# Four-token query runs, decay moved from keys to values, and another schedule in a fused linear-attention and sine-MLP kernel

## The chip, the cores and the metric

One core of a Trainium2 chip runs the whole program in one launch. The metric is device microseconds of that core, the median of several runs.

## The reference, cut to what matters

```python
# q, k, v: (4, 8, 768, 64) f32; lam: (8,)
for b in range(12):                                   # blocks of 64 tokens
    intra = einsum('bhic,bhjc->bhij', qb, kb) * Dmask # lam**(i-j) for i >= j, else 0
    intra = einsum('bhij,bhjd->bhid', intra, vb)
    inter = einsum('bhid,bhde->bhie', qb * lam**(pos+1), kv_state)
    out[block] = intra + inter
    kv_state = lam**64 * kv_state + einsum('bhsd,bhse->bhde', kb * lam**(63-pos), vb)
x = out as (3072 tokens, 512)
h = x @ w_in                                          # w_in (512, 2048)
g = h + sin(alpha*h)**2 / (alpha + 1e-9)
return g @ w_out                                      # (2048, 512), f32 out
```

## The kernel before, in words

**Tiling.** Attention runs in 24 blocks of 128 tokens (4 batches of 6), all 8 heads at once; the MLP in 6 chunks of 512 tokens, 4 blocks each. The decays are taken out of the score matrix: q is multiplied by `Lq` = lam to the token's place in its batch (L464), k by `Lk` = lam to minus that place (L471), so scores need a 0/1 mask only and the state needs no decay of its own. Both products go to bf16 into `qk2`; v is cast to `v2` (L473).

**Attention, per block s.** `piece_Q` (L506) and `piece_T` (L488) transpose q and k on TensorE (PE) through PSUM, and L511 and L493 copy them to `qkT`; from block `TD` = 12 on, a DMA transpose on SP's queue (L479) does both instead. `part_S` (L543) makes scores of all heads in two banks, DVE masks them into `Sm` (L552). `part_Z` (L568) accumulates the state in bank 7, copied to `Zc` (L583) or from block 12 on to the block-diagonal `Zd` (L578). `part_O` (L616 or L603, then L623) makes the output, copied to `xT` (L632), the MLP's input. q is loaded for two blocks at once, two neighbouring tokens of a head per partition, runs of 512 bytes; k and v in runs of 256 bytes.

**MLP.** A hidden unit (`unit_A`, L671, 4 matmuls of 512 columns; `unit_A2`, L705, two hidden tiles of 256 columns) fills a PSUM bank; ACT takes the sine (L681, L715), POOL or ACT the square (L686, L720 and L685, L719; one source line calls either engine), DVE adds (L688, L723) into `gT`. `unit_B` (L736) multiplies four hidden tiles by `w_out`; after four of them ACT copies the bank to `osb` (L749) and a store goes out (L751).

**Loads.** SP asks for q, k, v of blocks 0 to 3 first, then the first 512 columns of w_in in f32 into `ws`, which DVE casts (L391). The other three quarters of w_in and four quarters of w_out are cast by POOL's own DMA queue; `load_w1(i, [last["k32", 3]])` and the wait of `load_q(4, [last["w1", 2]])` tie them to the arrival of k of block 3, and of the third quarter of w_in (index 2). All loads are issued on line 342.

**Order.** `_Plan` records every operation with a cost and its tiles; `_settle` and `_order` choose for each engine an order (and an engine, where two are offered) by a list schedule over these costs, and `emit` writes the instructions with semaphores. PE may take any of the next 40 operations, SP only the next. A filler (`spin`, L829) multiplies unused data while PE would idle ahead of the first hidden unit.

Of the kernel before, what the change touches and what calls it, by code (L numbers as in the profile page):

```python
# [13 lines left out]
class _Op:  # L14


    def __init__(self, eng, emit, dur, reads, writes, dma, after, issue, lat, runs=64):
        self.eng, self.emit, self.dur = eng, emit, dur
        self.given = eng
        self.issue, self.lat, self.runs = issue, lat, runs  # L20
        self.lead = 0
        self.reads, self.writes, self.dma = reads, writes, dma
        self.port = False
        self.after = after
        self.deps = set()
        self.needed = False
        self.count = None
        self.start = None
        self.done = None
        self.knows = None  # L30


class _Plan:

    AHEAD = {"PE": 40, "SP": 1}
    SLACK = 0.3  # L40
    EARLY = 0.0, 0.0

    LAT = 0.2
# [10 lines left out]
    def op(self, eng, emit, dur, reads=(), writes=(), dma=None, after=(), issue=0.4, lat=2.6, runs=64):  # L54
# [14 lines left out]
        o.deps.discard(o)  # L69
        o.lead = self.lead  # L70
# [4 lines left out]
    def _transfers(order):  # L75
# [5 lines left out]
        left = {e: [[o.start + 0.8, o.runs, o.dur / o.runs, o] for o in sorted(q, key=lambda o: o.start)]  # L81
# [19 lines left out]
    def _settle(self):  # L101

        filler, lands, best = self.filler, {}, None
        for _ in range(8):
            self.filler = filler
            for o in self.ops:
                o.eng, o.start, o.done = o.given, None, None
            order = self._order(lands)
            new = self._transfers(order)
            off = sum(abs(t - o.done) for o, t in new.items())  # L110
            state = [(o, o.eng, o.start, o.done) for o in order]
            if best is None or off < best[0]:
                best = off, order, state
# [5 lines left out]
    def _order(self, lands):  # L119
        index = {o: i - o.lead for i, o in enumerate(self.ops)}  # L120
        left = {}
        for o in self.ops:
            left.setdefault(o.eng if isinstance(o.eng, str) else "any", []).append(o)
        fixed = {e: left.pop(e, []) for e in ("PE", "SP")}
        free = [o for e in left for o in left[e]]
        clock = {e: 0.8 for e in ("PE", "SP", "ACT", "DVE", "POOL")}
        wire = 0.0
        port = 0.0
        order = []

        def ready(o):
            t = 0.0
            for d in o.deps:
                if d.done is None:
                    return None
                t = max(t, d.done + (0.0 if d.eng == o.eng else self.LAT))
            return t

        while fixed["PE"] or fixed["SP"] or free:
            best = None  # L140
            for e in ("PE", "SP"):
                can = []
                for o in fixed[e][:self.AHEAD[e]]:
                    r = ready(o)
                    if r is not None:
                        can.append((max(r, clock[e]), index[o], o, e, o.dur))
                if can:
                    soon = min(c[0] for c in can)
                    soon += self.EARLY[1] if e == "PE" and soon < self.EARLY[0] else self.SLACK
                    c = min((c for c in can if c[0] <= soon), key=lambda c: c[1])  # L150
                    if best is None or c[:2] < best[:2]:
                        best = c
            for o in free:
                r = ready(o)
                if r is None:
                    continue
                if o.port:
                    r = max(r, port)
                if isinstance(o.eng, str):
                    c = (max(r, clock[o.eng]), index[o], o, o.eng, o.dur)  # L160
                else:
                    _, e, d = min((max(r, clock[e]) + d + late, e, d) for e, d, late in o.eng)
                    c = (max(r, clock[e]), index[o], o, e, d)
                if best is None or c[:2] < best[:2]:
                    best = c
            t, _, o, e, dur = best
            if e == "PE" and self.filler is not None:
                emit, reads, last = self.filler
                if last.start is not None:
                    self.filler = None  # L170
                else:
                    deps = [self.writer[b] for b in reads]
                    at = max([clock["PE"]] + [d.done + self.LAT if d.done is not None else t for d in deps])
                    n = int((t - at) / 0.4)
                    if n > 0:
                        f = _Op("PE", lambda h, n=n: emit(h, n), 0.4 * n, tuple(reads), (), None, (), 0, 0)
                        f.deps = set(deps)
                        f.start, f.done = at, at + 0.4 * n
                        order.append(f)
            if isinstance(o.eng, str):  # L180
                (fixed[e] if e in fixed else free).remove(o)
            else:
                free.remove(o)
                o.eng = e
            o.start = t
            if o.dma is not None:
                clock[e] = t + o.issue
                wire = max(wire, t + 0.8) + dur
                o.done = max(t + 0.8 + o.dur + o.lat, lands[o]) if o in lands else wire + o.lat
            else:  # L190
                clock[e] = o.done = t + dur
                if o.port and e != "ACT":
                    port = o.done
            order.append(o)
        return order
# [48 lines left out]
def bass_lightning_attn__then__act_snake_kernel(  # L244
# [26 lines left out]
    TD = 12  # L271
# [5 lines left out]
    RU = 4  # L277

    es = contextlib.ExitStack()
    with es:  # L280
# [18 lines left out]
        q32 = ring("q32", RL // 2, [128, H, 2, D], F32)  # L299
# [8 lines left out]
        mask = sb("mask", [128, 8, 128], BF16)  # L308
        maskf = sb("maskf", [128, 128], F32)
# [4 lines left out]
        E_i = sb("E_i", [128, 2 * NB, H], I32)  # L314
        E_f = sb("E_f", [128, 2 * NB, H], F32)
        lnL = sb("lnL", [128, 2 * NB, H], F32)
        Lq = sb("Lq", [128, NB, H], F32)
# [12 lines left out]
        def _(_unused_eng):  # L330
# [5 lines left out]
            P.EARLY = 20.0, 0.3  # L336
# [4 lines left out]
            def load(dst, src, key, dur, sem, eng="SP", lat=2.6, after=(), issue=0.4, runs=64):  # L341
# [3 lines left out]
            def load_q(s, after=()):  # L345
# [3 lines left out]
                for lo, hi in ((0, 4), (4, H)) if s < 4 else ((0, H),):  # L349
                    last["q32", s] = load(  # L350
                        q32[j][:, lo:hi, :, :].rearrange("p h t d -> p h (t d)"),
                        q[b, lo:hi, n * BL:(n + 2) * BL, :].rearrange("h (p t) d -> p h (t d)", t=2),
                        [("q32", j, a) for a in range(lo // 4, hi // 4)],
                        (0.9 if s == 0 else 1.1 if s < 4 else 2.3), f"q32{j}" + (str(lo) if s < 4 else ""),
                        lat=2.7, after=after, runs=8 * (hi - lo),
                    )

            def load_kv(s, which="kv"):
                b, n, j = s // NB, s % NB, s % RL
                for nm, src, dst in (("k32", k, k32), ("v32", v, v32)):  # L360
                    if nm[0] in which:
# [3 lines left out]
                            (nm, j), 1.1, f"{nm}{j}", lat=2.7,  # L365
# [7 lines left out]
            def load_w1(i, after):  # L373
# [3 lines left out]
                    [("w1", 2 * i), ("w1", 2 * i + 1)], 2.55, f"w1{i}", "POOL", 3.8, after, 0.8, 32,  # L377
                )

            def load_w1_first():  # L380
                for lo in (0, 256):
# [3 lines left out]
                        ("ws", lo), 1.65, f"ws{lo}", lat=2.7, runs=32,  # L385
# [8 lines left out]
            def load_w2(i, after):  # L394
# [3 lines left out]
                    [("w2", 2 * i), ("w2", 2 * i + 1)], 2.55, f"w2{i}", "POOL", 3.8, after, 0.8, 32,  # L398
# [3 lines left out]
            load(lam_bc[:, :], bass.AP(lam.tensor, 0, [[0, 128], [1, H]]), "lam", 0.1, "lam", "ACT", runs=1)  # L402
            load(alphaT[:, :], bass.AP(moe_alpha.tensor, 0, [[128, NM], [1, 128]]), "alphaT", 0.1, "alphaT", "ACT", lat=4.9, runs=1)
# [5 lines left out]
            load_q(2)  # L409
# [9 lines left out]
            op("POOL", lambda e: e.tensor_copy(E_f[:, :, :], E_i[:, :, :]), 0.3, ["E_i", "E_k"], ["E_f"])  # L419
# [5 lines left out]
            op("DVE", lambda e: e.memset(maskf[:, :], 1.0), 0.2, writes=["maskf"])  # L425
            op("POOL", lambda e: e.affine_select(
                out=maskf[:, :], in_=maskf[:, :], pattern=[[1, 2], [2, 64]], compare_op=ALU.is_ge,
                fill=0.0, base=0, channel_multiplier=-1), 0.5, ["maskf"], ["maskf"])
            op("DVE", lambda e: e.tensor_copy(mask[:, :, :], bass.AP(maskf, 0, [[128, 128], [0, 8], [1, 128]])),  # L429
               0.8, ["maskf"], ["mask"])  # L430

            for i in range(2):
# [3 lines left out]
            lnlam_b = bass.AP(lnlam, 0, [[H, 128], [0, 2 * NB], [1, H]])  # L436
            op("DVE", lambda e: e.tensor_tensor(lnL[:, :, :], E_f[:, :, :], lnlam_b, ALU.mult), 0.2,
               ["E_f", "lnlam"], ["lnL"])
            op("ACT", lambda e: e.activation(Lq[:, :, :], lnL[:, 0:NB, :], ACTF.Exp), 0.3, ["lnL"], ["Lq"])
            op("ACT", lambda e: e.activation(Lk[:, :, :], lnL[:, NB:2 * NB, :], ACTF.Exp, scale=-1.0), 0.3,  # L440
               ["lnL"], ["Lk"])
            op("ACT", lambda e: e.activation(warm[:, :], lnlam[:, 0:1], ACTF.Sin, scale=0.0), 1.5,
               ["lnlam", "Lk"], ["warm"])
# [7 lines left out]
            def QE(s, a):  # L451
                return "DVE" if (s, a) in () else "POOL"
# [5 lines left out]
            def scale_block(s):  # L458
# [3 lines left out]
                for a in range(2) if s % 2 == 0 else ():  # L462
                    ported(op(QE(s, a),
# [466 lines left out]
```

## Time and profile before

| | |
|---|---|
| runs | 222.61, 223.09, 224.41 us (median 223.09) |
| profiled run | 223.52 us, span 221.4 us, granted clock 1.00 |
| PE | busy 208.6 us, 94% of the span, 1645 matmuls |
| ACT, DVE, POOL | 155.9, 122.6, 89.1 us (70, 55, 40%) |
| DMA | 33.31 MB, mean 150 GB/s; 63520 packets under 512 B |
| PE idle | 5.6 us before 20 us, 4.6 us from there to the last matmul, 2.6 us after it |

Busy time counts instructions on the engine; a busy PE need not be at its peak. In the timeline each row is start, length, engine, line, operation, output and inputs, count, and in brackets the idle time ahead of it and what ended it. In the table of windows the columns are the stretch, its length, then busy time (and instructions) of PE, weight loads, DVE, ACT and POOL, the granted clock, the DMA share and GB/s.

### The profile page before, as it was taken

The numbers are of one execution on the slowest core, as the hardware profiler recorded it, in microseconds if no ns is written. First come the engines' busy times: TensorE is split into PE (matmuls) and PEld (weight loads), VectorE is DVE, ScalarE is ACT, GpSimd is POOL, SyncE is SP. The second block draws the span as 40 slices with busy tenths as digits, with TensorE's granted clock in tenths as the row PEclk, the third lists the DMA queues.
The fourth block names the chain that finished last, engine by engine and source line by source line (L and its number), as shares of the span: only waits on it lengthen the run. The fifth ranks groups of instructions, "written<-read, shape, count | busy, mean of one in ns | idle before, by whom it ended". The sixth has DMA issues, their size and how long they took to land.

```text
span 221.4 us, 4062 instructions
## 1 busy us (share of the span) xinstructions
PE 208.6 (94%) x1645; PEld 110.7 (50%) x1645; DVE 122.6 (55%) x184; ACT 155.9 (70%) x277; POOL 89.1 (40%) x100
## 2 busy tenths in 40 slices
PE   3889987899898999999999999999999999999995
PEld 1446433456575785545445444545545444444444
DVE  4687775354777887667655455645465544445100
ACT  3735994347697997788788887877788677778211
POOL 4386763454978776863576103011001011110100
DMA  5999999999999999999999752110110011101112
GB/s 131 236 232 271 206 214 208 217 235 237 233 245 275 242 191 245 219 254 189 276 240 245 155 112 33 47 50 0 47 50 21 26 47 50 47 0 49 75 70 95
DMA packets 83651, 33.31 MB, mean 150 GB/s; under 512 B 63520, under 2 KB 80688, under 8 KB 83632
## 3 DMA queue, kind: packets, MB, share of 16 engines
q1 hardware_dynamic: 76880, 24.25, 53.6%
q0 software_dynamic: 3696, 3.67, 9.9%
q10 hardware_dynamic: 3056, 5.13, 6.4%
q8 instruction: 13, 0.21, 0.4%
q14 instruction: 6, 0.05, 0.1%
HBM read 27.28 MB, written 6.29 MB: 152 GB/s over the span
## 4 chain that ended last, share of the span: by engine, by line
PE 63%; DMA 24%; POOL 4%; SPq 4%; ACT 2%; DVE 1%; issue 1%
PE bank L736 32%; PE bank L671 24%; DMA k<-in_k_dram 10%; DMA q<-in_q_dram 5%; DMA v<-in_v_dram 4%; DMA w<-in_moe_w_in_dram 4%; SPq L342 4%; PE bank L705 3%; PE bank L623 2%; PE bank L543 2%; POOL qk L471 1%; POOL qk L464 1%; PE bank L603 1%; POOL u L720 1%; DVE gT L723 1%
## 5 line engine op out<-in xcount | busy, mean ns | idle before, releaser
L736 PE MATMUL bank<-w,gT 128*128 128x512 bf16 (+1 forms) x400 | 94.8, 371 | 0.0
L688 DVE SCALAR_TENSOR_TENSOR gT<-u,rinv,bank 128x512 bf16<-128x512 bf16 x74 | 54.6, 746 | 51.7 <-ACT u L685 34.2
L671 PE MATMUL bank<-xT,w 128*128 128x512 bf16 x296 | 74.2, 379 | 0.6 <-DVE gT L688 0.6
L681 ACT ACTIVATE t<-bank,alpha 128x512 bf16<-128x512 f32 x74 | 50.6, 686 | 24.1 <-PE bank L671 24.0
L736 PEld LDWEIGHTS bank<-w,gT 128*128 128x128 bf16 x400 | 37.7, 98 | 39.6
L686 POOL TENSOR_TENSOR u<-t 128x512 bf16<-128x512 bf16 x19 | 19.7, 1040 | 80.7 <-ACT t L681 79.7
L671 PEld LDWEIGHTS bank<-xT,w 128*128 128x128 bf16 x296 | 28.5, 98 | 34.9 <-DVE gT L688 1.1
L685 ACT ACTIVATE u<-t 128x512 bf16<-128x512 bf16 x55 | 34.4, 629 | 1.8 <-DVE gT L723 0.3
L552 DVE TENSOR_TENSOR Sm<-bank,mask 128x1024 bf16<-128x1024 f32 x24 | 29.2, 1222 | 10.3 <-PE bank L568 7.7
L464 POOL TENSOR_TENSOR qk<-q,Lq 128x512 bf16<-128x512 f32 x24 | 24.5, 1044 | 21.7 <-DMA q<-in_q_dram 18.1
L471 POOL TENSOR_TENSOR qk<-k,Lk 128x512 bf16<-128x512 f32 x22 | 22.9, 1044 | 7.2 <-DMA k<-in_k_dram 7.0
L749 ACT COPY osb<-bank 128x512 f32<-128x512 f32 (+1 forms) x25 | 14.2, 569 | 14.8 <-PE bank L736 14.8
L705 PE MATMUL bank<-xT,w 128*128 128x256 bf16 x176 | 22.3, 273 | 2.0 <-DVE gT L723 2.0
L723 DVE SCALAR_TENSOR_TENSOR gT<-u,rinv,bank 128x256 bf16<-128x256 bf16 x44 | 19.1, 476 | 7.2 <-POOL u L720 4.1
L715 ACT ACTIVATE t<-bank,alpha 128x256 bf16<-128x256 f32 x44 | 18.5, 471 | 3.3 <-PE bank L705 3.1
L705 PEld LDWEIGHTS bank<-xT,w 128*128 128x128 bf16 x176 | 16.2, 98 | 5.5 <-DVE gT L723 3.0
L473 ACT CAST v<-v 128x512 bf16<-128x512 f32 x18 | 11.0, 615 | 7.6 <-DMA v<-in_v_dram 7.6
L632 ACT CAST xT<-bank 128x512 bf16<-128x512 f32 (+1 forms) x18 | 12.9, 716 | 2.8 <-PE bank L568 1.6
L720 POOL TENSOR_TENSOR u<-t 128x512 bf16<-128x512 bf16 x11 | 11.3, 1039 | 4.7 <-ACT t L715 4.6
L543 PE MATMUL bank<-qkT 64*128 64x128 bf16 x192 | 9.8, 226 | 0.2 <-DVE qkT L493 0.2
L623 PE MATMUL bank<-Sm,v 128*64 128x128 bf16 x192 | 9.9, 225 | 0.0
L829 PE MATMUL bank<-mask,ident 128*128 128x512 bf16 x12 | 5.7, 564 | 3.7 <-DVE mask L429 3.7
(55 smaller groups left out, 111.4 us busy)
## 6 DMA issues: line engine op xcount, KB each, us to landing
k<-in_k_dram SPq DMA_DIRECT2D x24, 256.0 KB, 5.5
v<-in_v_dram SPq DMA_DIRECT2D x24, 256.0 KB, 5.5
q<-in_q_dram SPq DMA_DIRECT2D x10, 512.0 KB, 5.5
out_dram<-osb ACTq DMA_DIRECT2D x19, 256.0 KB, 2.0
w<-in_moe_w_out_dram POOLq DMA_DIRECT2D x4, 512.0 KB, 13.1
w<-in_moe_w_in_dram POOLq DMA_DIRECT2D x3, 512.0 KB, 9.0
q<-in_q_dram SPq DMA_DIRECT2D x4, 256.0 KB, 4.6
ws<-in_moe_w_in_dram SPq DMA_DIRECT2D x2, 512.0 KB, 5.4
```

Of the source, the lines that this page charges most:

```text
L464: lambda e, a=a: e.tensor_tensor(qk2[:, j:j + 2, 4 * a:4 * a + 4, :], q32[jq][:, 4 * a:4 * a + 4, :, :].rearrange("p h t d -> p t h d"), b ...
L471: lambda e: e.tensor_tensor(qk2[:, j, H:2 * H, :], k32[jl][:, :, :], lk, ALU.mult), 0.7 if s in (0,1) else 1.05,
L552: op("DVE", lambda e: e.tensor_tensor(Sm[s % 2][:, :, :], banks[:, 512 * b0:512 * b0 + 1024].rearrange("p (c i) -> p c i", i=128), mask[:, ...
L671: ins = e.matmul(ps[hb][:, c0:c1], w1[:, kc, 128 * m:128 * (m + 1)], xT[x][:, kc, c0:c1], start=(kc == 0 and c0 == lo), stop=(kc == NKC - ...
L681: op("ACT", lambda e: e.activation(t16[ju][:, w], ps[hb][:, w], ACTF.Sin, scale=alpha[:, m:m + 1]), 0.69 * f, [bank(hb), "alpha"], [("t16" ...
L685: lambda e: (e.activation(u16[ju][:, w], t16[ju][:, w], ACTF.Square) if e is nc.scalar else e.tensor_tensor(u16[ju][:, w], t16[ju][:, w], ...
L686: e.tensor_tensor(u16[ju][:, w], t16[ju][:, w], t16[ju][:, w], ALU.mult)), 0,
L688: op("DVE", lambda e: e.scalar_tensor_tensor(out=gT[g][:, m, w], in0=u16[ju][:, w], scalar=rinv[:, m:m + 1], in1=ps[hb][:, w], op0=ALU.mul ...
L705: ins = e.matmul(ps[hb][:, 256 * i:256 * i + 256], w1[:, kc, 128 * (m + i):128 * (m + i + 1)], xT[x][:, kc, lo:lo + 256], start=(kc == 0 a ...
L715: op("ACT", lambda e, i=i: e.activation(t16[ju][:, 256 * i:256 * i + 256], ps[hb][:, 256 * i:256 * i + 256], ACTF.Sin, scale=alpha[:, m + ...
L723: op("DVE", lambda e, i=i: e.scalar_tensor_tensor(out=gT[g][:, m + i, lo:lo + 256], in0=u16[ju][:, 256 * i:256 * i + 256], scalar=rinv[:, ...
L736: ins = e.matmul(ps[ob][:, w], gT[g][:, m, 128 * s4:128 * (s4 + 1)], w2[:, m, w], start=(m == 0), stop=(m == NM - 1),)
```

## The change

q of blocks 0 to 3 is loaded in two pieces of four heads for all four blocks, four neighbouring tokens per partition (runs of 1024 bytes); its own decay table `Lq4`, its own mask, and strides of four in scores and outputs follow. DVE multiplies these four blocks' q. From block 4 on, and for blocks 0 and 1, the decay `Lk` goes into v and k is only cast; blocks 2 and 3 keep it in k. `TD` goes from 12 to 10. The mask is stored once and read with a stride of zero over the 8 heads. The fillers use 256 columns of a tile set at the start. The planner gets other costs, hand-over times by engine, windows of choice by engine, and a list of priority shifts; the four stores of chunk 0 are recorded later, after the pieces of blocks 8 to 11. The three w_in requests of POOL stand in one run, as before.

```diff
-    AHEAD = {"PE": 40, "SP": 1}
-    SLACK = 0.3
-    LAT = 0.2
+    AHEAD = 40
+    WINDOW = {"PE": 0.3, "ACT": 0.1, "DVE": 0.1, "POOL": 0.1}
+    PIPE = {"ACT": 0.11, "DVE": 0.09, "POOL": 0.045, "PE": 0.0}
+    HOP = {"PE": 0.055, "ACT": 0.035, "DVE": 0.035, "POOL": 0.075, "SP": 0.1}
+    DRAIN = 0.085
+    MOVES = (
+        (500, 10, "all", -75), (367, 10, "all", -265), (210, 3, "all", -185), (249, 30, "all", 55),
+        (294, 3, "ACT", 60), (111, 1, "SP", -10), (239, 30, "all", -40), (396, 1, "SP", 5),
+        (94, 10, "SP", -10), (244, 1, "ACT", -20),
+    )
...
+        prio = {o: i - o.lead for i, o in enumerate(self.ops)}
+        for at, width, kind, by in self.MOVES:
+            for o in self.ops[at:at + width]:
+                if (kind == "all" and o.given != "SP") or o.given == kind or ...:
+                    prio[o] += by
...
-    TD = 12
+    TD = 10
+    QD = ((0, 0), (0, 2), (1, 0), (1, 2))
...
+                if s < 4:
+                    for a in range(2):
+                        last["q32", s] = load(
+                            q32[:, a, :, :, :].rearrange("p (h x) t d -> p h (x t d)", x=2),
+                            q[0, 4 * a:4 * a + 4, 0:4 * BL, :].rearrange("h (p t) d -> p h (t d)", t=4),
+                            [("q32", a, 0), ("q32", a, 1)], 1.66, f"q32{a}", lat=1.4, after=after, runs=32,
+                        )
+                    return
...
-            load_q(2)
...
+                if s == 0:
+                    for a in range(2):
+                        for t in (0, 2):
+                            ported(op(QE(a, t),
+                               lambda e, a=a, t=t: e.tensor_tensor(
+                                   qk2[:, t:t + 2, 4 * a:4 * a + 4, :],
...
-                ported(op("DVE" if s in (0,1) else "POOL",
-                   lambda e: e.tensor_tensor(qk2[:, j, H:2 * H, :], k32[jl][:, :, :], lk, ALU.mult), 0.7 if s in (0,1) else 1.05,
-                   [("k32", jl), "Lk"], [("k2", j)]))
-                op((("ACT", 0.62, 0.0), ("POOL", 1.05, 0.3)) if s > 11 else "ACT", lambda e: ... v2[j] <- v32[jl] ...
+                plain, decayed = ((kj, k32[jl], ("k32", jl), ("k2", j)), (vj, v32[jl], ("v32", jl), ("v2", j)))[::1 if s < 2 or s > 3 else -1]
+                ported(op("POOL", lambda e: e.tensor_tensor(decayed[0], decayed[1][:, :, :], lk, ALU.mult), 1.05,
+                          [decayed[2], "Lk"], [decayed[3]]))
+                op((("ACT", 0.62, 0.0), ("POOL", 0.62, 0.3)) if s > 11 else "ACT",
+                   lambda e: (e.copy if e is nc.scalar else e.tensor_copy)(plain[0], plain[1][:, :, :]), 0.62,
+                   [plain[2]], [plain[3]])
...
+            def queries(s):
+                nq = 4 if s < 4 else 2
+                w = BL // nq
+                return s % RT // nq * nq, nq, slice(w * (s % nq), w * (s % nq) + w)
...
-                    for ahead in range(s + 2, min(s + 3, NBLK)) if s >= 10 else ():
+                    for ahead in range(s + 2, min(s + 3, NBLK)) if s >= 8 else ():
...
             piece_Q(0, 4)
+            piece_Q(2, 6)
...
-            piece_Q(2, 4)
...
-                    ins = e.matmul(ps[0][:, :], ident[:, :], mask[:, 0:4, :].rearrange("p a b -> p (a b)"))
+                    ins = e.matmul(ps[0][:, 0:256], idle[:, 0:128], idle[:, :])
...
-            load_pair(10)
...
-            for st in stores:
-                if st is not None:
-                    st("SP")
             pieces = pieces_of(8, None, False) + pieces_of(10, 9, False)
...
             prep(13)
+            for st in stores:
+                if st is not None:
+                    st("SP")
```

More of the change, by code (lines that the diff above doesn't have):

```diff
@@ L101, in _settle @@
     def _settle(self):
[L103 to L111, printed above, removed]
+        prio = {o: i - o.lead for i, o in enumerate(self.ops)}
+        for at, width, kind, by in self.MOVES:
+            for o in self.ops[at:at + width]:
+                if (kind == "all" and o.given != "SP") or o.given == kind or (kind == "any" and not isinstance(o.given, str)):
+                    prio[o] += by
+        lands, best = {}, None
+        for _ in range(10):
+            order, new, off = self._pass(prio, lands)
             if best is None or off < best[0]:
-                best = off, order, state
+                best = off, order, [(o, o.eng, o.start, o.done) for o in order]
+            if off < 0.5:
+                break
             lands = new
@@ L117, in _settle, with _pass @@
         return best[1]
[L119 to L121 removed]
+    def _pass(self, prio, lands):
         for o in self.ops:
[L123 to L168 removed]
@@ L194, in _order @@
             order.append(o)
+            can.discard(o)
+            left -= 1
+            for s in after.get(o, ()):
+                waits[s] -= 1
+                if not waits[s]:
+                    can.add(s)
         return order
@@ L835, in _ @@
                 if i == 0:
[L836 removed]
+                    P.filler = (spin, ("idle",), u)
                 if i == 3:
```

260 lines of the change are left out of this document (164 added, 96 removed).

## The prediction

> **What bounds the kernel now.** I read the busy tenths first, then TensorE's (PE's) waits, then the chain that ended last, then the timeline at the places these name. The busy tenths give two stages.
>
> ```profile
> PE   3889987899898999999999999999999999999995
> DMA  5999999999999999999999752110110011101112
> ```
>
> One digit is 5.5 us. PE is full from the fifth digit on except for dents near 36 and 55 to 66 us, while the DMA engines are saturated until about 120 us. So the end is a sum of PE work, and time can only go where PE still waits, or where PE work itself goes. The waits of PE between 19 and 100 us are these (us in total, times, longest):
>
> ```profile
> PE bank L705 <- DVE gT L723: 2.0, 3, 1.0
> PE bank L506 <- POOL qk L464: 1.7, 1, 1.7
> PE bank L671 <- DVE gT L688: 0.6, 1, 0.6
> PE bank L488 <- POOL qk L471: 0.2, 1, 0.2
> ```
>
> 4.5 us in all. The chain shows what stands behind the second and fourth (start, us, what):
>
> ```profile
> 9.09 5.78 DMA k<-in_k_dram
> ...
> 14.93 1.04 POOL qk L471
> 15.97 0.88 POOL w L342
> 16.85 9.00 DMA w<-in_moe_w_in_dram
> ...
> 26.28 16.12 DMA k<-in_k_dram
> ```
>
> k of block 3 lands at 14.93, POOL scales it, only then asks for w_in; the second w_in part lands at 25.85, only then SP asks for q, k, v of blocks 4 and 5, and those crawl behind the weight loads. PE meets that at 39.31:
>
> ```profile
> 16.80 2.35 DVE L552 TENSOR_TENSOR Sm<-bank,mask 128x1024 bf16<-128x1024 f32 x2
> 19.89 1.92 PE L705 MATMUL bank<-xT,w 128*128 128x256 bf16 x16
> 38.21 2.04 POOL L464 TENSOR_TENSOR qk<-q,Lq 128x512 bf16<-128x512 f32 x2 [2.23 <-DMA q<-in_q_dram]
> 39.31 0.40 PE L506 MATMUL bank<-ident,qk 128*128 128x128 bf16 x4 [1.72 <-POOL qk L464]
> ```
>
> The first MLP matmul (L705) starts at 19.89, right after the last score mask on DVE (16.80 to 19.15). From 90 us PE does not wait, so the last 130 us are PE work alone.
>
> **Parts of the change, one by one.**
>
> *q of blocks 0 to 3 in 1 KB runs.* The same 1 MB, 1024 packets for 2048. In the trace's packet records a 512 B packet took 31 ns in the mean, and ws (w_in's first columns, 1 KB packets) 55 ns, at the fast end 46. Over 16 engines: 2048 x 31 / 16 = 3.97 us against 1024 x 46..55 / 16 = 2.94 to 3.5 us, so 0.45 to 1.0 us of engine time. Packets overlap (busy shares of about 1.2 in these windows), so elapsed 0.4 to 0.85; I take 0.65. k3, ws and w_in all stand behind these q loads in the queue and land so much earlier. The price: k0 now stands behind 1 MB of q, not 0.5 MB, some 1.7 us later; the queue has paid that back by k2, because q of blocks 2 and 3 was in front of it before.
>
> [...]
>
> *Work moved between engines in the head.* DVE now scales q of blocks 0 to 3 (four 128x512 operations). The row for this shape on DVE is L471, two of them: 0.68 us, and 1.31 while POOL ran one. POOL keeps v0, v1, k2, k3 (4 x 1.04), and is idle until v0 lands, near 10 us, so I take 0.68. Lq for four tokens is there at about 6.9 (before: 6.4; DVE's alpha copy now stands ahead of the exponent product, which waits for alphaT, landed at 5.4). DVE then: 4 x 0.68 + two q copies at 0.69 + k copy 0.42 + Sm pair 2.36 + Zc 0.43 + xT 0.73 + k copy 0.42 + Sm pair 2.35 = 10.8, ending at 17.7, with some 0.7 of hand-overs to PE 18.4. By k3 it is: 16.80 - 0.65 + 2.35 = 18.5. Before: 19.15. So the first MLP matmul moves from 19.89 to about 19.2; with two operations at 1.31 it would be 0.6 later than now. The casts of k0 and k1 go to ACT (2 x 0.62), idle there after its tables. The extra iota, mask and memset lie before the lam load lands at 4.6. Fillers of half the size start at about 1 us for 3.66; they fill PE idle time only.
>
> *Decay in v from block 4 on.* POOL still does one 1.04 us scaling a block, of v; ACT (some blocks POOL) casts k where it cast v, 0.62. Instruction for instruction the same cost. k's transposes wait for 0.62 instead of 1.04, and v is needed later than k.
>
> *w_in "in one go".* In the instruction order of both kernels POOL issues the three w_in loads in a row, behind k3. Nothing moves but the 0.65 above.
>
> *The order around block 4.* Before, PE runs 52 L671-type matmuls after the first two units' L705, and 16 of L736, ahead of the first q transpose of block 4; the changed order has 56 and 20. Eight more at 0.216 (0.86 per 4 in the chain) are 1.73 us of work that must be done anyway and now stands before the wait. q of block 4 lands at 38.21 - 0.65 and is scaled one POOL operation later, so PE may pass at 38.66. PE gets there at 37.59 - 0.7 + 1.73 = 38.6 (with the 0.57 wait of L671 kept). At that point the kernel is 0.65 + 1.73 = **2.4 us ahead**. The bounds: 1.7 (q no earlier) to 3.2 (q earlier by 0.85 and the 0.57 gone too).
>
> *Blocks 10 and 11 transposed by DMA (TD 12 to 10).* 96 PE transposes become 80: 16 x 0.055 (0.22 for 4) = **0.9 us** of PE work. Two more DMA transposes on SP, 2.3 us each at the median to issue. Behind them on SP stand k and v of block 13 and the four stores of chunk 0, which before were out at 62.6. They are needed near 80; see rivals.
>
> *The waits of L705 at 59 to 85 (2.0 us).* One is shown in the chain: ACT stood for v of block 8 (57.16), with the square and so gT behind it. The changed order puts the k cast of block 8 after four MLP units instead, near the time k lands; k of block 9 is asked for ahead of k6, which delays k6 by 1.2 us, inside the 2 us it has. Between 0 and 2.0 I take **1.0**.
>
> *Squares to ACT.* POOL's squares go from 30 to 11, ACT's from 66 to 85: 19 x 0.63 = 12 us on ACT, Zd copies 13 to 19, 6 x 0.36 = 2.2. Of these 13 squares lie after 90 us. There ACT has:
>
> ```profile
> 90.00:110.00 20.00, 20.00 (x164) 10.32 (x163) 12.48 (x19) 16.06 (x30) 11.29 (x13) 1.00 1.18 230
> 110.00:130.00 20.00, 19.93 (x154) 9.88 (x153) 11.27 (x14) 17.10 (x30) 9.30 (x11) 1.00 0.91 187
> ```
>
> (fourth busy column ACT). From 90 to 175 it is 68.2 of 85 us; with 7 squares and 6 copies more 74.8, 88%. At 17.1 of 20 PE lost 0.07 us, so the load alone costs little. I put 0.4 for new waits here and at the stores; bounds 0 and 6.
>
> **Sum.** The profiled run took 223.5 us (span 221.4 and 2.1 around it): 223.5 - 2.4 - 0.9 - 1.0 + 0.4 = 219.6. The median of the three runs, 223.1, is 0.4 under the profiled one, so **219.2 us**. Own range: all bounds at their best 3.2 + 0.9 + 2.0 give 217.0; at their worst 1.7 + 0.9 + 0 - 0.4 give 220.9.
>
> **Rivals.**
> 1. *The loads take it back.* The saturated DMA lets PE wait again at blocks 6 to 9: k6 1.2 us later, PE 2.4 us earlier. For it: saturation to 120 us, and POOL's 18.1 us of waits for q. Against it: from block 6 on a pair of blocks has about 17 us of PE work and needs 1.5 MB, 6.6 us at 230 GB/s. If the 2.4 and 1.0 are lost, only 0.9 stays: 222.2.
> 2. *The stores come late.* ACT's osb copy of chunk 1 waits for the store of chunk 0, now behind both transposes of blocks 12 and 13 on SP (near 79; a store there lands after 2 to 5 us). ACT arrives near 81.5. At worst 3 us of ACT, 2 of them PE's: 221.2.
> 3. *Slower: ACT becomes the bound from 90 to 175 us.* With all squares on ACT, a block's burst (xT 0.73, Zd 0.72, cast 0.62, osb 0.59) delays the sine, hence gT, hence the next of the three hidden-unit banks. The bank has about 2 us to spare; if each of the 12 blocks overruns by 0.5, 6 us are lost: 225.2. It decides from 4 / 12 = 0.33 us a block. For it: 88% of an in-order engine. Against: the row at 17.1 of 20.
>
> The w_in part that does nothing is already counted at nothing.
>
> **Chances.** Forecast 0.62, loads 0.16, stores 0.07, ACT 0.15. The loads and the stores end within 1% (about what a measurement here can tell from no change, 220.9 to 225.3), ACT at or beyond its edge. Faster by over 1%: 0.62, within 0.23, slower 0.15. The range for 8 in 10 reaches from the forecast's best, 217.0, over the loads case to just short of the ACT case: 224.0.
>
> **What the profile after would show.** First MLP matmul near 19.2, w_in asked for near 15.3, q of block 4 transposed near 38.7 after a PE wait under 0.5; 80 PE transposes; PE waits between 45 and 90 under 1.5 us; no PE wait from 90 us on, with ACT near 17.7 of 20. Wrong would be: PE waits on sine or gT after 90 us (rival 3), an ACT wait for an out transfer near 82 (rival 2), k or q waits at blocks 6 to 9 (rival 1), or DVE's q scalings at 1.31 and the first MLP matmul after 19.9.

## The result, and the profile after

The changed kernel takes 225.08 us in the median (223.61 to 229.55, 20 runs), the kernel before beside it 223.74 us (222.61 to 225.14, 20 runs). The ratio is 1.0051, with a 95% interval of 1.0027 to 1.0075: some 1.1 us slower (0.5%), where 219.2 us were forecast. All ratios here leave out runs that lie more than 1.5% above the fastest of their kernel (of the kernels with the change or parts of it 3 of 20 here, 5 of 12 in run 3 below, 2 of 12 in run 5, 4 of 12 in run 12); medians and ranges are of all runs. The profiled run took 223.98 us (span 222.1, granted clock 0.992).

The busy tenths of the page after, with the granted clock between them:

```profile
PE   7898989999999598999999999999999999999995
PEclk9999999999999969999999999999999999999999
DMA  4999999979989999999999991110110111101112
```

The early dents of TensorE (PE) are mostly gone; there is a new one in the slice from 72 to 78 us, and in the slice behind it, up to 83 us, stands the only digit of the clock that is not 9. The waits of PE after (us in total, times, longest):

```profile
PE bank L602 <- DMA qkT<-qk: 2.6, 1, 2.6
...
PE bank L731 <- DVE gT L748: 1.0, 1, 1.0
PE bank L676 <- ACT xT L692: 0.6, 1, 0.6
...
PE bank L765 <- DVE w L424: 0.4, 1, 0.4
```

L602 are the scores, L731 and L765 the hidden units, L676 the product of q with the state (before: L543, L671, L705, L616). The 1.7 us at block 4 are gone, and the 2.0 us of the hidden units but for 0.2. A wait of 2.6 us for a DMA transpose has come. The timeline of PE at the places that the prediction named:

```profile
20.59 1.92 PE L765 MATMUL bank<-xT,w 128*128 128x256 bf16 x16 [0.44 <-DVE w L424]
...
40.23 0.39 PE L558 MATMUL bank<-ident,qk 128*128 128x128 bf16 x4
...
77.92 0.40 PE L602 MATMUL bank<-qkT 64*128 64x128 bf16 x8 [2.62 <-DMA qkT<-qk]
...
79.14 3.45 PE L765 MATMUL bank<-xT,w 128*128 128x256 bf16 x16
```

The first hidden units start at 20.59 (before 19.89, forecast 19.2). q of block 4 is transposed at 40.23 without a wait. At 75.3 PE is ready for the scores of block 10 and stands until 77.92. The 16 matmuls that follow then take 3.45 us; the same 16 took 1.92 at 20.59. The table of windows shows why (columns: stretch, length, PE busy and instructions, granted clock, DMA share, GB/s):

```profile
79.00:80.00 1.00, 1.00 (x15) 0.50 1.28 279
80.00:81.00 1.00, 1.00 (x6) 0.50 1.35 218
81.00:82.00 1.00, 1.00 (x7) 0.50 1.39 212
82.00:83.00 1.00, 1.00 (x18) 0.84 1.08 243
```

PE runs at half clock from about 78.9 to 82.3 us, 3.4 us, which is 1.7 us of work lost. With the wait that is 4.3 us; the profiled 223.98 less 4.3 is 219.7. That this is near the forecast's sum for a profiled run (219.6) is partly luck: a head that came late and hidden units that waited less than forecast nearly cancel (see the part on why the prediction was wrong). What PE stood for is on SP's queue (start, us; a row lasts while the queue is held):

```profile
65.25 1.37 SPq L370 DMA_DIRECT2D k<-in_k_dram  x1
66.66 1.41 SPq L370 DMA_DIRECT2D v<-in_v_dram  x1
68.19 3.85 SPq L531 DMA_TRANSPOSE qkT<-qk  x1
72.09 0.57 SPq L370 DMA_DIRECT2D k<-in_k_dram  x1
72.70 0.58 SPq L370 DMA_DIRECT2D v<-in_v_dram  x1
73.33 2.18 SPq L531 DMA_TRANSPOSE qkT<-qk  x1
75.56 0.58 SPq L370 DMA_DIRECT2D q<-in_q_dram  x1
```

The transpose of block 10 holds SP for 3.85 us. Behind it stand k and v of block 13, then the transpose of block 11, and behind that the loads of block 14. The scores of block 10 read q of both blocks, so they wait for the second transpose.

From 90 us on PE does not wait: the two windows that the prediction showed read, after,

```profile
90.00:110.00 20.00, 20.00 (x163) 10.11 (x162) 12.44 (x18) 17.89 (x35) 11.24 (x13) 1.00 1.21 254
110.00:130.00 20.00, 20.00 (x156) 9.98 (x154) 10.30 (x13) 17.19 (x32) 7.86 (x9) 1.00 1.25 230
```

with ACT (fourth busy column) at 17.89 and 17.19 of 20 us and PE at 20.00.

### The profile page after: what moved, and what is told of

Read it like the earlier page. It is cut to its first block, busy times and chain, and to the rows that moved or that the text cites. A ratio compares the mean times of both kernels' runs of the same rounds, so it can differ in the third digit from the quotient of the medians.

```text
span 222.1 us, 4152 instructions
## 1 busy us (share of the span) xinstructions
PE 212.5 (96%) x1684; PEld 115.4 (52%) x1684; DVE 120.1 (54%) x181; ACT 165.9 (75%) x301; POOL 68.8 (31%) x82
## 2 busy tenths in 40 slices
DMA packets 84707, 33.84 MB, mean 152 GB/s; under 512 B 65600, under 2 KB 81744, under 8 KB 84688
## 4 chain that ended last, share of the span: by engine, by line
PE 74%; DMA 11%; ACT 6%; SPq 5%; POOL 1%; issue 1%; DVE 1%; POOLq 0%
PE bank L796 36%; PE bank L731 26%; DMA k<-in_k_dram 6%; SPq L370 5%; PE bank L765 4%; DMA ws<-in_moe_w_in_dram 3%; PE bank L683 3%; PE bank L602 2%; DMA qkT<-qk 2%; ACT t L775 2%; ACT t L741 1%; PE bank L663 1%; POOL u L746 1%; PE bank L676 1%; ACT qk L525 1%
## 5 line engine op out<-in xcount | busy, mean ns | idle before, releaser
L731 PE MATMUL bank<-xT,w 128*128 128x512 bf16 x296 | 74.2, 379 | 1.0 <-DVE gT L748 1.0
L731 PEld LDWEIGHTS bank<-xT,w 128*128 128x128 bf16 x296 | 28.3, 98 | 35.3 <-DVE gT L748 1.8
L745 ACT ACTIVATE u<-t 128x512 bf16<-128x512 bf16 x69 | 43.5, 630 | 2.4 <-DVE gT L783 0.4
L522 POOL TENSOR_TENSOR v<-v,Lk 128x512 bf16<-128x512 f32 x22 | 23.0, 1044 | 26.2 <-DMA v<-in_v_dram 26.2
L515 POOL TENSOR_TENSOR qk<-q,Lq 128x512 bf16<-128x512 f32 x20 | 20.5, 1044 | 16.0 <-DMA q<-in_q_dram 16.0
L765 PE MATMUL bank<-xT,w 128*128 128x256 bf16 x176 | 23.1, 285 | 0.6 <-DVE w L424 0.4
L765 PEld LDWEIGHTS bank<-xT,w 128*128 128x128 bf16 x176 | 17.0, 102 | 4.3 <-DVE w L424 0.6
L692 ACT CAST xT<-bank 128x512 bf16<-128x512 f32 (+1 forms) x18 | 14.1, 796 | 0.4 <-PE bank L683 0.4
L889 PE MATMUL bank<-idle 128*128 128x256 bf16 x67 | 12.4, 325 | 1.3 <-DVE idle L454 1.3
L525 ACT CAST qk<-k 128x512 bf16<-128x512 f32 x15 | 9.3, 618 | 4.5 <-DMA k<-in_k_dram 4.5
L602 PE MATMUL bank<-qkT 64*128 64x128 bf16 x192 | 9.5, 219 | 2.6 <-DMA qkT<-qk 2.6
L779 ACT ACTIVATE u<-t 128x512 bf16<-128x512 bf16 x16 | 10.1, 644 | 0.2
L602 PEld LDWEIGHTS bank<-qkT 64*128 64x128 bf16 x192 | 5.4, 94 | 8.3 <-ACT u L779 3.1
```

What stands on the lines that cost most here:

```text
L515: lambda e, a=a: e.tensor_tensor(qk2[:, j:j + 2, 4 * a:4 * a + 4, :], q32[:, jq, 4 * a:4 * a + 4, :, :].rearrange("p h t d -> p t h d"), b ...
L522: ported(op("POOL", lambda e: e.tensor_tensor(decayed[0], decayed[1][:, :, :], lk, ALU.mult), 1.05, [decayed[2], "Lk"], [decayed[3]]))
L602: ins = e.matmul(ps[(b0, b1)[h]][:, 128 * jp:128 * (jp + 1)].rearrange("p (t x) -> p t x", t=nq), qkT[r, jt, 4 + jp, :], qkT[r, jq:jq + nq ...
L731: ins = e.matmul(ps[hb][:, c0:c1], w1[:, kc, 128 * m:128 * (m + 1)], xT[x][:, kc, c0:c1], start=(kc == 0 and c0 == lo), stop=(kc == NKC - ...
L745: lambda e: (e.activation(u16[ju][:, w], t16[ju][:, w], ACTF.Square) if e is nc.scalar else e.tensor_tensor(u16[ju][:, w], t16[ju][:, w], ...
L765: ins = e.matmul(ps[hb][:, 256 * i:256 * i + 256], w1[:, kc, 128 * (m + i):128 * (m + i + 1)], xT[x][:, kc, lo:lo + 256], start=(kc == 0 a ...
```

## The experiments

Eleven kernels ran, each timed in five rounds beside the kernel before. They bear the numbers of their labels (there is no run 8), which the expectations use too. Line numbers differ by some 5 to 25 from kernel to kernel.

### Runs 1 to 4: what the transposes of blocks 10 and 11 cost

Run 1 puts these transposes back on PE; the list of priority shifts is made to hit the same operations. The planner orders all engines anew over it, so PE, ACT, DVE and POOL also run some other operations around blocks 8 to 12 in another order.

```diff
-    TD = 10
+    TD = 12
```

> The changed kernel with blocks 10 and 11 transposed on TensorE again (TD 12), the priority shifts kept on the same operations. Theory A (the loss sits at block 10: its scores need both DMA transposes, which SP issues late behind loads; the wait of 2.6 us then costs 1.65 us more at half clock): the wait and the half clock go, 0.9 us of TensorE transposes come back: 225.1 - 4.3 + 0.9 = 221.7 (221.0 to 222.5), clock 1.00, no TensorE wait over 0.8 us between 70 and 90 us. Theory B (blocks 8 to 11 are late because the loads are late on saturated DMA, whoever transposes): the scores of block 10 wait all the same, for k or q of block 10: 224.5 to 226.

222.66 us (221.26 to 224.14); ratio 0.9958 (0.9925 to 0.9992); granted clock of the profiled run 1.00. The longest wait of PE between 20 and 200 us is now

```profile
PE bank L736 <- DVE gT L753: 0.6, 1, 0.6
```

Without the DMA transposes of two blocks the changed kernel is 0.9% quicker than with them, and quicker than the kernel before, although PE has 16 transposes more to do.

Run 2 keeps them on SP, but moves them ahead of the loads that stand in front of them.

```diff
-  ... q12 k12 v12 T10 k13 v13 T11 q14 ...        (SP's order)
+  ... T10 T11 k13 v13 q12 k12 v12 q14 ...
```

> The changed kernel with one thing moved: on SP the two DMA transposes of blocks 10 and 11 go ahead of the loads of q, k, v of block 12 and k, v of block 13. Theory A: the transposes are issued near 66 and 69 instead of 68 and 73, land before 75, and the 2.6 us wait with its half clock goes; the five loads are 4 to 5 us later, so the scores of block 12 may wait, up to 3 us: 221 at best, 224.5 at worst. Theory B: no transposed block earlier, since its k is late: 225 or more.

228.70 us (226.25 to 229.33); ratio 1.0205 (1.0162 to 1.0248). The transposes are out by 71.1, but the scores of block 10 start later still. Timeline of POOL, ACT and PE:

```profile
77.87 2.04 POOL L525 TENSOR_TENSOR qk<-q,Lq 128x512 bf16<-128x512 f32 x2 [6.60 <-DMA q<-in_q_dram]
79.04 0.62 ACT L535 CAST qk<-k 128x512 bf16<-128x512 f32 x1 [5.96 <-DMA k<-in_k_dram]
79.83 0.73 ACT L702 CAST xT<-bank 128x512 bf16<-128x512 f32 x1
...
80.61 0.61 PE L612 MATMUL bank<-qkT 64*128 64x128 bf16 x8 [3.99 <-ACT xT L702]
```

Now q and k of block 12 are late. ACT stands 5.96 us in front of the cast of k12 (79.04), and the copy of xT that PE needs comes after it on ACT (79.83). In both orders of SP's queue something is late: in the change the second transpose (issued at 73.33), here q and k of block 12 (POOL stands 6.60 us for q, ACT 5.96 for k). Not all of the loss is this order's: the profile of run 2 also has a late head (first hidden units at 22.51 us, in the profile after at 20.59) and runs at half clock from 79.7 to 86.5 us.

Run 3 leaves the wait at block 10 but keeps PE busy in it.

```diff
+    20 matmuls of the constant tile into an unused bank, ahead of the scores of block 10
```

> The changed kernel with 20 matmuls of 256 unused columns on TensorE ahead of the scores of block 10, in the place of its wait; their output is overwritten. Theory A (the half clock from 79 to 82.4 us follows from TensorE standing idle for 2.6 us): the wait is filled, the clock stays 1.00, the 16 matmuls behind it take 1.8 us and not 3.4: 225.1 - 1.6 = 223.5 (223.0 to 224.2). Rival C (the half clock comes by itself, from power or at random): no change, 225.1, clock below 1.00 in some runs.

225.58 us (223.87 to 229.09); ratio 1.0034 (1.0001 to 1.0068), no better than the change itself (1.0051). The profiled run kept its clock, and the 16 matmuls took 1.92 us, but in that run the first hidden units started at 23.80 (in the profile after at 20.59), so PE came to block 10 only at 77.7, and how much waiting its 2.3 us of fillers replaced can't be read. Nothing is settled by it but this: the head of the changed kernel varies, and what it loses is partly got back later (3.2 us late in the head, 0.5 us at the end).

Run 4 does that one part alone, in the kernel before.

```diff
-    TD = 12
+    TD = 10
```

> The kernel before with one part of the change alone: blocks 10 and 11 transposed by DMA (TD 10), order replanned by its own planner. Theory A: 0.9 us of TensorE transposes go, but SP, which has the four stores ahead there, issues the second transpose near 75, it lands near 79, and the scores of block 10 wait some 2 to 3 us, with the half clock if over about 2.5: 224.5 to 227. Theory B: 222.8, faster by the transposes.

226.40 us (224.87 to 227.93); ratio 1.0125 (1.0081 to 1.0168). With 0.9 us less PE work the kernel before is 2.8 us slower (1.25%). Here PE stands for xT and not for a transpose, 1.62 us at 82 and 1.52 at 89 us:

```profile
81.99 1.05 PE L705 MATMUL bank<-xT,w 128*128 128x256 bf16 x8 [1.62 <-ACT xT L632]
```

The mean granted clock is 0.977, with half clock from 83.2 to 86.6 us, behind this wait, and also from 14.9 to 21.7 us in the head, where the order of PE is that of the kernel before and the first hidden units start at 21.58 instead of 19.89. So the 2.8 us may be partly chance; the two of the six runs with a clock of 1.00 took 224.87 and 226.01 us.

### Runs 5 to 7: the head

By the packet records, the last packets of lambda and alphaT moved by 4.2 and 5.5 us in the profiles of before, after and runs 1 and 4, but at 6.5 and 7.7 us in those of runs 2 and 3. DVE's exponent product, which q's scaling needs, stands behind the alpha copy in the changed order. Runs 5 and 6 load q of blocks 0 to 3 in packets of 512 bytes again, in the changed kernel and in run 1.

```diff
-    q[0, 4a:4a+4, 0:4*BL, :]   four heads, four tokens: 1 KB runs
+    q[0, :, 2x of every 4 tokens, :]   eight heads, two tokens: 512 B runs
```

> The changed kernel, but q of blocks 0 to 3 is read in packets of 512 bytes (each load takes two tokens of all eight heads in place of four tokens of four heads); the result in SBUF is the same. Theory S (small loads starved): lambda (128 packets of 32 bytes) and alphaT (16 of 512 bytes) stand on ACT's queue; where SP's queue with its 1 KB packets happens to start first, they come through only at 6.5 and 7.7 us (in the two profiles where that happened) and not at 4.1 and 5.4, which makes the exponent product and the q scaling behind the alpha copy 2.2 us later. With 512 byte packets both have landed by 4.3 and 5.2 us whichever queue starts first, as in the kernel before. The wait at block 10 stays. So the runs lie between 223.3 and 225.5 us, none above 226, median 224.3 (the changed kernel: 225.08, up to 229.55); the larger packets' own gain, which the prediction put at 0.65 us, is lost, which is in these numbers. Rival R (the late landing is chance, with nothing of the packet size in it): the same spread as the changed kernel, median 225 to 226, some runs above 227.

> The changed kernel with the transposes of blocks 10 and 11 on PE again (as in the first experiment, 222.66 us, 221.26 to 224.14) and with q of blocks 0 to 3 in packets of 512 bytes. Theory S: the upper half of that experiment's runs (222.9 to 224.1) were those with lambda and alphaT late; without them 221.3 to 222.7, median 221.9, granted clock 1.00. Rival R: 222.7 again, up to 224 or more. If the 1 KB packets are worth more than their side effect, it is above 222.7.

Run 5: 224.91 us (223.25 to 227.14), ratio 1.0038 (1.0007 to 1.0068). Run 6: 223.17 us (221.35 to 224.24), ratio 0.9966 (0.9937 to 0.9995). In the profile of run 6 the small loads were late all the same (alphaT's last packet at 7.4 us):

```profile
8.44 0.17 DVE L491 COPY alpha<-bank 128x16 f32<-128x16 f32 x1 [4.83 <-PE bank L489]
```

(in the profile after the same copy starts at 6.44). So theory S falls: the packet size does not decide whether the small loads are late, and run 5 has two runs above 226 us where it forecast none. The two runs give something else: against 1.0051 and 0.9958 with 1 KB packets, the small packets cost −0.3 and +0.2 us, each give or take 1, so nothing that can be told apart.

Run 7 takes run 1, with 1 KB packets, and asks for lambda on SP ahead of q.

```diff
-    load(lam_bc, ..., "ACT", ...)
+    load(lam_bc, ..., "SP", ...)
```

> The changed kernel with the transposes of blocks 10 and 11 on PE again and with the lambda load on SP's queue ahead of q, so that alphaT is the only load at the head of ACT's queue; q keeps its 1 KB packets but is asked for some 0.5 us later. Theory S: lambda lands by 3.5 us, alphaT by 4.5 us in every run; the late half of the runs is gone; against the early runs of the first experiment q's later start costs up to 0.5 us, so 221.3 to 222.6, median 221.9. Rival R: no better than the first experiment, 222.7 plus up to 0.5.

221.60 us (220.54 to 222.48); ratio 0.9901 (0.9861 to 0.9940): the quickest kernel of all, 1.0% under the kernel before. alphaT's last packet moves at 3.5 us, and DVE's copy of alpha starts at 5.53:

```profile
5.53 0.17 DVE L491 COPY alpha<-bank 128x16 f32<-128x16 f32 x1 [1.92 <-PE bank L489]
```

Asking for lambda first was worth 1.3 us against run 1 (0.57%, give or take 0.5%). That this is the price of late small loads is argued: only one execution of each kernel has a profile, so how often they are late isn't known, and they now come sooner than in the profile of run 1 too. The six runs lie within 1.9 us, but run 12 below, with the same edit, spreads over 6.2.

### Runs 9 to 12: which resource, and whose fault

Run 9 is the changed kernel with only lambda moved; run 10 is the kernel before with that edit; run 11 is run 9 with 24 constant matmuls ahead of the scores of block 10.

> The changed kernel with the lambda load on SP's queue ahead of q (alphaT alone at the head of ACT's queue), and the transposes of blocks 10 and 11 on SP as in the change. Theory F (a floor): the transposes for block 10 land at a time that SP's queue sets, 77.7 us in the profile after, so an earlier head only makes TensorE wait longer there: 3.0 to 3.8 us in place of 2.6, half clock behind it, and the late runs vanish; 223.3 to 225.0 us, median 224.0, none below 223.0. Rival H (the head decides): the wait stays near 2.6 us and the head's gain passes to the end, 1.1 us as from the first experiment to the seventh, so that the quickest run is near 222.5 and the median 223.5 to 224.0.

> The kernel before with the lambda load on SP's queue ahead of q and nothing else moved by hand. Theory F: in the kernel before the exponent product stands ahead of the alpha copy and TensorE waits 1.7 us for q of block 4 at 39 us anyway, so what the head gains or loses is taken up there: 223.7 us, within 0.5 of the kernel before. Rival H: the small loads come late at random in both kernels alike, and the kernel before gains 1.0 us too: 222.7; then that landing is no part of the difference between the two kernels.

> The kernel of the ninth run with 24 matmuls on constant data (2.8 us at full clock) ahead of the scores of block 10, so that TensorE is busy while it waits for the transposes; they are dropped from the result. Theory F with the clock as a term of its own: the wait shrinks to below 1.0 us, the granted clock stays 1.00 and the 16 matmuls behind the scores take 1.92 us and not 3.45, so 1.5 to 1.7 us under the ninth run: 222.4. Rival W (only the wait itself counts, the half clock is made up by what runs beside it): the same as the ninth run within 0.5, or slower by what the 24 matmuls outlast the wait.

Run 9: 223.76 us (222.77 to 225.12), ratio 1.0006 (0.9982 to 1.0030). Run 10: 223.72 us (222.84 to 225.42), ratio 1.0008 (0.9983 to 1.0033). Run 11: 226.19 us (225.52 to 226.83), ratio 1.0116 (1.0084 to 1.0147).

The kernel before gains nothing from an earlier lambda, the changed one gains 0.45% (1.0 us, give or take 0.8). So by these ratios it is the change that made the kernel sensitive to the two small loads. Run 9's median lies in the forecasts of both theories, so the time doesn't choose between them; the profile shows that theory F is wrong in its detail: the time at which the transposes land is no fixed floor. In run 9 they are issued 2 us sooner and PE waits 1.3 us at block 10, but two others now come late:

```profile
75.78 0.40 PE L602 MATMUL bank<-qkT 64*128 64x128 bf16 x8 [1.30 <-ACT u L779]
...
99.88 0.40 PE L663 MATMUL bank<-qkT,Zd 128*128 128x128 bf16 x4 [1.17 <-DMA qkT<-qk]
...
110.02 0.38 PE L663 MATMUL bank<-qkT,Zd 128*128 128x128 bf16 x4 [1.66 <-DMA qkT<-qk]
```

These 4.1 us are about the 4.3 that the profile after lost at block 10: PE is ahead of SP's queue, and meets it somewhere between blocks 10 and 15. Run 7, without the two transposes, waits 0.55 us there. Run 11 missed: its clock stayed at 1.00 through block 10, but its profile shows a wait of 1.9 us for w in the head, transposes issued 1.7 us later than in run 9, and a half-clock stretch at 103.6; how much of its 2.4 us over run 9 the matmuls cost isn't settled, and the price of the half clock alone stays open.

Run 12 tells SP's queue from the link to the scores. It is run 7, every engine in the same order, with the two DMA transposes issued on SP all the same, into a buffer that nothing reads. It is the cleanest of these experiments, since no engine's order moves.

```diff
+    T10 ahead of k13, T11 ahead of q14, on SP: scr <- qk   (PE transposes both blocks as in run 7)
```

> The kernel of the seventh run (lambda first, blocks 10 and 11 transposed on PE: 221.6 us) with the two DMA transposes of blocks 10 and 11 issued on SP all the same, at the places that they have in the changed kernel, into a buffer that nothing reads; the order of every engine is otherwise that of the seventh run. Theory Q (SP's queue): what costs is the 4 to 6 us that the two instructions hold SP's queue, which makes the loads and the transposes of blocks 12 to 15 behind them late: 223.2 to 224.0 us, near the 223.76 of the ninth run, with waits for qkT near 100 and 110 us. Theory L (the link): what costs is that the scores of block 10 hang on the transposes of two blocks, and that TensorE has nothing in their place to do: within 0.5 us of the seventh run, 221.3 to 222.1.

224.79 us (222.59 to 228.81); ratio 1.0026 (0.9992 to 1.0059), against 0.9901 for run 7. Two instructions whose result nobody reads cost 1.25%, 2.8 us (give or take 1.2), with no PE work saved in return. Theory L, within 0.5 us of run 7, falls. Theory Q holds in the main: the ratio gives 223.9 us, in its range (the median of all runs is above it), but the waits for qkT that it expected near 100 and 110 us don't show under that name (PE waits 1.04 us at 109.75, put down to gT). The path can be read in the timeline of run 12:

```profile
73.44 0.58 SPq L395 DMA_DIRECT2D q<-in_q_dram  x1
...
78.20 2.04 POOL L540 TENSOR_TENSOR qk<-q,Lq 128x512 bf16<-128x512 f32 x2 [2.57 <-DMA q<-in_q_dram]
...
80.20 1.04 POOL L805 TENSOR_TENSOR u<-t 128x512 bf16<-128x512 bf16 x1
81.27 1.66 DVE L808 SCALAR_TENSOR_TENSOR gT<-u,rinv,bank 128x256 bf16<-128x256 bf16 x4 [2.92 <-POOL u L805]
...
82.98 1.05 PE L790 MATMUL bank<-xT,w 128*128 128x256 bf16 x8 [2.12 <-DVE gT L808]
```

and beside it in run 7:

```profile
71.36 0.98 SPq L375 DMA_DIRECT2D q<-in_q_dram  x1
...
76.94 2.04 POOL L520 TENSOR_TENSOR qk<-q,Lq 128x512 bf16<-128x512 f32 x2 [0.75 <-DMA q<-in_q_dram]
```

q of block 14 is asked for 2.1 us later and lands 1.3 us later. POOL stands 2.57 us in front of its scaling (0.75 in run 7); the multiplication that makes u comes next on POOL (80.20), gT starts after u (81.27), and PE stands 2.12 us for gT. So the wait that PE shows (gT here, qkT in the change, xT in run 2) names the last engine of a chain that begins on SP's queue; for xT in run 4 this isn't shown. In run 12 the two instructions hold SP for 3.65 and 2.50 us, in a stretch where ACT (1.66 us for a k, up to 79.32), POOL (2.57 for q) and, through u and gT, PE (2.12) all hang on the next load.

One rival stays in part: the two transposes also bring 512 KB of packets to the DMA engines (33.84 MB in the profile after, 33.31 in run 1). For q of block 14 the later request explains more than the whole delay, since from the request to POOL's scaling it took 4.8 us, in run 7 5.6. Whether busy DMA engines lengthen the time for which a transpose holds SP isn't shown; the last three transposes of the profile after, behind all loads, still hold it for 6.36 us, 2.1 each.

## Why the prediction was wrong, step by step

**Blocks 10 and 11 by DMA: −0.9 forecast, +2.1 to +2.8 measured (the change against run 1, run 9 against run 7, run 4).** This is the step that failed. The PE work did go (0.9 us), but the prediction put the price at nothing: it has "2.3 us each at the median to issue" and adds no wait for it. It doesn't work out when PE needs these two blocks (its "They are needed near 80" reads as said of the loads and stores behind them): PE was ready for the scores of block 10 at 75.3, and they hang on both blocks' transposes, the second of which was issued at 73.33. And SP was held as if it were free: the loads behind it are what ACT and POOL wait for (in run 2 ACT 5.96 us for k of block 12, in run 12 POOL 2.57 for q of block 14). Run 12 measures this side alone, 2.8 us, so some 1.9 net of the 0.9. Rival 1 was near: the loads did take the gain back, though at blocks 10 to 15 and not at 6 to 9, and as far as run 12 shows through later requests on SP rather than through slower transfers.

**The head: 19.2 forecast, 20.59 measured.** DVE's four scalings took 2.50 us (forecast 2.72), so that row stood. The second pair of masks did not: it started at 16.77, where 16.80 - 0.65 was forecast. After:

```profile
14.69 1.05 POOL L522 TENSOR_TENSOR qk<-k,Lk 128x512 bf16<-128x512 f32 x1 [0.16 <-DMA k<-in_k_dram]
15.12 1.30 DVE L692 CAST xT<-bank 128x512 bf16<-128x512 f32 x1 [0.52 <-PE bank L683]
16.77 2.35 DVE L611 TENSOR_TENSOR Sm<-bank,mask 128x1024 bf16<-128x1024 f32 x2
18.36 0.62 ACT L525 CAST v<-v 128x512 bf16<-128x512 f32 x1 [1.81 <-DMA v<-in_v_dram]
19.84 0.69 DVE L424 CAST w<-ws 128x1024 bf16<-128x1024 f32 x1 [0.72 <-DMA ws<-in_moe_w_in_dram]
```

and before:

```profile
17.23 0.62 ACT L473 CAST v<-v 128x512 bf16<-128x512 f32 x1 [0.52 <-DMA v<-in_v_dram]
...
19.07 0.68 DVE L391 CAST w<-ws 128x1024 bf16<-128x1024 f32 x1
```

Two rows of the sum were off. The loads behind q did not land 0.65 us sooner: k of block 3 came 0.24 us sooner (14.69 against 14.93), v of block 3 over 1 us later, and ws, which landed 6.7 us after it was asked for (before 5.3 to 5.6), so late that PE waited 0.44 us for w after the masks. And the copies to xT of these four blocks, taken at 0.73 us, took 1.30: they now write with a step of four elements, not two. Lambda and alphaT, loads of 4 and 8 KB, were not late in this profile (last packets at 4.0 and 5.4 us). In others they were, and the prediction took them at their times in one profile of before, while the change put the alpha copy ahead of the exponent product. Run 9 against the change puts an earlier lambda at 1.0 us, and run 10 shows no such gain in the kernel before. Even with it the first hidden units start at 20.09 in run 9 and 19.91 in run 7, so it does not give the 19.2 either.

**1 KB packets: −0.65 forecast, nothing seen.** Packet for packet the records did show it (512 B in 27 to 31 ns, 1 KB in 46 to 55), but runs 5 and 6 with the small packets are level with their partners (1.0038 beside 1.0051, 0.9966 beside 0.9958), each pair to about 1 us. As far as these two pairs can tell, the lower of the forecast's bounds (q no earlier) was the better choice.

**The wait at block 4: 1.73 forecast, held.** Eight more matmuls stand ahead of the transposes of block 4 and the 1.72 us wait is gone. Of the 2.4 us that the kernel should be ahead there, 0.8 were left (40.23 against 39.31 + 1.73), since the head was 1.4 us later than forecast and the wait for gT at 31.58 grew from 0.57 to 0.95.

**The waits of the hidden units: −1.0 forecast, −1.8 measured** (L705 before, 2.0 us, to L765 after, 0.2).

**ACT as the bound, and the stores: refuted in this profile.** PE does not wait from 90 us on, with ACT at 17.9, 17.2 and 17.5 of 20 us (the third from 130 to 150). PE shows no wait for the stores either.

**The sum comes out, in part by luck.** The forecast was 219.2 / 223.09 = 0.983 of the kernel before. Without the terms for the packets (0.65 us) and the transposes (0.9) it is 0.990. Run 7, which has neither the two DMA transposes nor the late small loads, measured 0.9901. So what is left of the forecast is worth 1% together, the transposes cost 1.05% of it back (run 9 against run 7) and the small loads another 0.45%. The agreement to the last digit is luck: each ratio is uncertain by 0.2 to 0.4%, and the profile of run 7 has a head 0.7 us later than forecast and a wait of 2.4 us at 32.4 that no term has, against more gained at the hidden units than forecast.

## What to carry to other kernels

Before work is moved from a busy engine to a DMA queue, read what stands behind it on that queue and which engine waits for the next load there; here a transpose that took 0.45 us from PE cost 1.1 to 1.4 us of the end, through engines that never touch its result. Work out when a moved result is needed from the changed schedule, and from every tile that its first reader takes. A load of a few KB at the head of a kernel deserves a place at the front of a queue when a chain hangs on it (run 9 against the change: 1.0 us, give or take 0.8); where none did, in run 10, it won nothing. A step in the output of a copy belongs in its price (here 1.30 us where 0.73 was taken).

## What the hardware showed that was not expected

In the profile after a DMA transpose of one block holds SP's queue for 1.23 to 3.85 us (14 of them, at the median 2.51), in the profile of before for 1.36 to 3.10 (12, 2.32). In the profile after a load of 256 KB right behind one mostly holds it for 0.56 to 0.58 (once 1.07); elsewhere in the queue such loads hold it for up to 6.25 us (v, at 27.09).

A copy of 128x512 from PSUM to bf16 took 1.30 us on DVE and 1.31 on ACT where it wrote with a step of four elements (8 bytes), and 0.73 and 0.74 with a step of two (the change at 15.12 and 13.65 us; before, the same two engines).

The half clock follows no plain rule of the length of the wait. A wait of PE of 2.62 us (the change, block 10), of 1.88 (run 11, at 103), of 1.82 (run 5, at 110.9) and of 1.62 (run 4, at 82.0) were each followed by 3.4 us at half clock; one of 2.68 (run 3, at 8.4), of 2.41 (run 7, at 32.4), of 2.12 (run 12, at 83.0) and of 1.72 (before, at 39.3) were not. So no run shows the 2.5 us from which run 4's forecast expected it: half clock came after 1.62 in run 4 and not after 2.68 in run 3. The half-clock stretches lasted 3.4 us (the change, runs 5 and 11, run 4 from 83.2) or 6.8 us (run 2 from 79.7, run 4 from 14.9). What sets it off stays open.

Two loads of 4 and 8 KB on ACT's queue moved their last packets by 4.2 and 5.8 us in some profiles and at 5.9 to 6.5 and 7.4 to 7.7 in others. In the three late profiles (runs 2, 3 and 6) SP's queue moved its first packet before ACT's, at 1.9 against 3.0 to 3.2 us; in the profile of before it did too (1.92 against 2.58), and there nothing was late. What decides it stays open.
